# Shifted slices for the previous block's keys, and DMA copies for its values, in a fused attention and MLP kernel

## The chip, the cores and the metric

The kernel runs on one core of a Trainium2 chip. The metric is device time in microseconds (us) of one execution. A ratio is from the fast runs of both kernels in the same rounds, so it is not quite the ratio of the medians quoted beside it. Brackets hold a 95% interval. Where a ratio is turned into us, it is multiplied by 217.

The engines are called PE (matmuls), DVE (VectorE), ACT (ScalarE), POOL (GpSimd) and SP (SyncE, which here only issues DMAs). A profile is one execution, with its own span; its times differ a little from the medians.

## The reference

The kernel computes windowed attention with global keys, and a two-layer MLP over its result.

```python
# q, k, v: (4, 8, 768, 64); 8 global keys; a window of 96 keys
rel = pos[:, None] - pos[None, :]
is_global = pos[None, :] < n_global
is_local = (rel >= 0) & (rel < n_local)
dist = where(is_global & ~is_local, n_local, abs(rel))
scores = q @ k.T / sqrt(64) - slopes * dist        # -1e9 outside global and local
a = softmax(scores)
x = (a @ v)                                        # -> (3072, 512)
h = x @ w_in                                       # (512, 2048)
g = s * relu(h) ** 2 + b
out = g @ w_out                                    # (2048, 512), f32
```

## The kernel before

The work is cut into 12 granules of 256 tokens, three for each batch element (granules 0, 1, 2 are batch element 0; granules 0, 3, 6 and 9 are first in theirs). A granule is two blocks of 128 queries. A block needs its own 128 keys, and the keys of the block in front of it. The 8 global keys are put into that second set, in place of 8 keys that no query of the block can reach. So for each granule that is not the first of its batch element, DVE builds two patched copies: `koff` (keys, transposed) and `voff` (values, with a column of ones).

```python
def make_koff(j, blocks=range(GB), ...):
    ...
    copy(ko[:, i0:i0+n, hs, :], t[:, 0, r0+i0:r0+i0+n, hs, :])
    nc.vector.tensor_copy(ko[:, i0:i0+n, hs, 0:NG],
        t[:, 0, 0, hs, 0:NG].unsqueeze(1).to_broadcast((P, n, nh, NG)))

def make_voff(j, blocks=range(GB), ...):
    ...
    copy(vo[:, i0:i0+n, :, :], vn[:, r0+i0:r0+i0+n, :, :])        # L349
    for i in blocks:
        nc.vector.tensor_copy(vo[0:NG, i, :, :], vn[0:NG, 0, :, :])  # L353
```

The keys and queries of granules 4 and later are transposed by DMAs on SP's queue, four a granule. Everything is put in order by hand. This is the part around granules 4 and 5, which the argument is about; `p1` and `p2` are the two MLP layers, `scores(s)` are score matmuls, and `stage_A(u)` are value matmuls of one pair of heads (granule 4 has u = 16 to 19).

```python
# ... granule 2 and granule 3
qk_by_dma(4); load_scalars()
# ...
stage_A(11)
# ...
qk_by_dma(5)          # four transposes on SP's queue, each after its load
r0, q0 = p1_mm(2, 5)
r0()
stage_A(14)
stage_A(15, ps_h)
q0()
make_koff(4)
# ...
run(scores(8))        # granule 4's first scores
make_voff(4)
p2_mm(2, 0, 0, FC // 2)
# ...
step(8, ...)          # holds stage_A(16), the first reader of granule 4's voff
```

The softmax here doesn't subtract the row's maximum and nothing guards it: scores larger than these inputs give would overflow.

## Time and profile before

The kernel takes 216.85 us (median; 216.78 to 217.0).

| | before |
|---|---|
| span of the profiled run | 215.4 us |
| PE busy | 209.8 us (97%) |
| DVE busy | 140.5 us (65%) |
| time PE waited for anything | 2.1 us, 1.9 of it before 5.1 us |
| DVE work that the change takes out | 14.6 us |

First, the page of the kernel before: its span, the busy us of each engine, and three rows of digits. Each digit is a fortieth of the span, in tenths; PEclk is the clock granted to PE, and DMA the busy share of the 16 DMA engines.

```profile
span 215.4 us, 4939 instructions
...
PE 209.8 (97%) x2013; PEld 143.8 (67%) x2013; DVE 140.5 (65%) x344; ACT 113.6 (53%) x175; POOL 67.0 (31%) x89
...
PE   6999999999999999999999999999999999999993
...
PEclk9999999999999999999999999999999999999999
DMA  5999999999999997999999949952310310311102
```

PE is busy from end to end, and the DMA engines are full for the first half.

The waits of PE (the instruction that waited and what released it, us in total, times, longest) say the same. This is all that the view lists:

```profile
PE ps_w L155 <- DVE idle L145: 1.2, 1, 1.2
PE ps_t L269 <- DVE nat L233: 0.7, 1, 0.7
PE ps_av L446 <- DVE xn L420: 0.2, 1, 0.2
```

The DVE work that the change removes, from the groups of instructions (line, operation, operands, shapes and count; then busy us and the mean ns of one; then the idle time before):

```profile
L353 DVE COPY voff<-vb 8x528 bf16<-8x528 bf16 x16 | 4.8, 330 | 0.3
L349 DVE COPY voff<-vb 128x1056 bf16<-128x1056 bf16 (+1 forms) x9 | 4.2, 464 | 0.0
L330 DVE COPY koff<-qk 128x1024 bf16<-128x1024 bf16 (+1 forms) x9 | 3.5, 390 | 0.0
...
L333 DVE COPY koff<-qk 128x64 bf16<-128x64 bf16 (+1 forms) x9 | 2.1, 234 | 0.3
```

The place where granule 4's values are first read, in the chain that ended last (start, us, what). PE goes from one piece to the next with no gap:

```profile
64.97 1.83 PE ps L611 x8
66.80 0.24 PE ps_av L446 x8
67.05 1.76 PE ps L566 x16
```

And two stretches as sums (the busy us and instructions of each engine, the mean granted clock, the DMA share, which is not used here, and GB/s):

```profile
68.70:74.70 6.00, 5.96 (x56) 3.65 (x56) 4.57 (x12) 3.62 (x5) 1.21 (x2) 1.00 2.05 158
74.70:81.50 6.80, 6.80 (x75) 4.94 (x74) 4.18 (x10) 4.17 (x6) 0.00 (x0) 1.00 1.69 177
```

### The profile page before, as it was taken

What the parts mean: (1) busy time and instruction counts of PE and PEld (TensorE: products, weight loads), DVE (VectorE), ACT (ScalarE), POOL (GpSimd) and SP (SyncE); (2) the same over time, 40 slices, a digit from 0 to 9 for tenths busy, and PEclk for the clock granted to TensorE, in tenths of its full rate; (3) what the DMA queues carried; (4) which work ended last, traced back from release to release, by engine and by line L of the source; (5) the groups of instructions that cost most, each with busy time, mean ns of one, the idle gap of its engine ahead of it and who ended that gap; (6) DMA issues with size and microseconds to landing.
All of it is one profiled execution on the core that took longest, in us unless ns stands there. A gap on an engine that the chain in (4) does not pass through costs nothing.

```text
span 215.4 us, 4939 instructions
## 1 busy us (share of the span) xinstructions
PE 209.8 (97%) x2013; PEld 143.8 (67%) x2013; DVE 140.5 (65%) x344; ACT 113.6 (53%) x175; POOL 67.0 (31%) x89
## 2 busy tenths in 40 slices
PE   6999999999999999999999999999999999999993
PEld 2578885557866575776676676676676676665852
DVE  3497579995989668985675675666676663432421
ACT  4675668585975564554644643544644642240610
POOL 8873335897646104506318045000000000000000
PEclk9999999999999999999999999999999999999999
DMA  5999999999999997999999949952310310311102
GB/s 166 197 177 206 207 206 173 152 152 127 117 150 138 157 183 110 156 255 171 208 133 171 171 79 159 132 102 72 97 50 5 97 52 24 73 52 49 49 3 97
DMA packets 107079, 27.33 MB, mean 127 GB/s; under 512 B 97712, under 2 KB 104112, under 8 KB 107056
## 3 DMA queue, kind: packets, MB, share of 16 engines
q0 software_dynamic: 72864, 12.85, 82.2%
q1 hardware_dynamic: 33136, 13.64, 34.5%
q10 hardware_dynamic: 1056, 0.52, 0.9%
q8 instruction: 16, 0.26, 0.5%
q14 instruction: 7, 0.06, 0.1%
HBM read 27.26 MB, written 6.29 MB: 156 GB/s over the span
## 4 chain that ended last, share of the span: by engine, by line
PE 91%; DVE 5%; DMA 2%; issue 0%
PE ps L566 38%; PE ps L611 35%; PE ps_s L395 5%; PE ps_av L446 5%; DMA first<-in_k_dram 2%; PE ps_2c L668 2%; DVE pt L411 1%; PE ps_t L269 1%; PE ps_s L372 1%; PE ps_w L155 1%; PE ps_s L468 1%; PE ps_x L542 1%; PE ps_t L301 1%; DVE o_early L644 1%; DVE wsum L589 1%; DVE xn L420 1%
## 5 line engine op out<-in xcount | busy, mean ns | idle before, releaser
L576 ACT ACTIVATE gT<-ps 128x512 bf16<-128x512 f32 x96 | 57.0, 598 | 76.4 <-PE ps L566 76.4
L566 PE MATMUL ps<-xT,w_in_bf 128*128 128x256 bf16 x768 | 90.2, 273 | 0.0
L611 PE MATMUL ps<-w_out_bf,gT 128*128 128x512 bf16 x368 | 83.9, 380 | 0.0
L566 PEld LDWEIGHTS <-w_in_bf 128*128 128x128 bf16 x768 | 72.7, 98 | 8.9
L611 PEld LDWEIGHTS <-gT 128*128 128x128 bf16 x368 | 34.4, 98 | 39.2
L579 DVE TENSOR_TENSOR gT<-gT 128x512 bf16<-128x512 bf16 x96 | 40.4, 424 | 24.2 <-ACT gT L576 22.2
L404 ACT ACTIVATE pt<-ps_s 128x1024 bf16<-128x1024 f32 (+1 forms) x44 | 39.2, 948 | 6.4 <-PE ps_s L395 6.4
L411 DVE TENSOR_TENSOR pt<-pt,tmpl 128x1024 bf16<-128x1024 bf16 (+1 forms) x40 | 25.6, 650 | 9.3 <-ACT pt L404 8.6
L104 POOL DMA_DIRECT2D nat<-in_k_dram x22 | 19.7, 895 | 8.1 <-DMA w_in_bf<-in_moe_w_in_dram 3.0
L104 POOL DMA_DIRECT2D nat<-in_q_dram x22 | 19.6, 891 | 8.3 <-DMA w_out_bf<-in_moe_w_out_dram 3.4
L105 POOL DMA_DIRECT2D vb<-in_v_dram x22 | 19.8, 900 | 5.7 <-DMA w_out_bf<-in_moe_w_out_dram 2.1
L420 DVE TENSOR_TENSOR xn<-ps_av,rc 128x256 bf16<-128x256 f32 x48 | 20.4, 425 | 1.7
L622 DVE SCALAR_TENSOR_TENSOR o_sb<-ps,s_bc,bvec 128x512 f32<-128x512 f32 x19 | 14.1, 744 | 9.9 <-PE ps L611 9.9
L446 PEld LDWEIGHTS <-pt 128*128 128x128 bf16 x320 | 14.6, 97 | 5.9 <-DVE xn L420 0.8
L419 DVE RECIPROCAL rc<-ps_av 128x4 f32<-128x4 f32 x48 | 8.5, 178 | 14.8 <-PE ps_av L446 13.5
L446 PE MATMUL ps_av<-vb,pt 128*128 128x65 bf16 x208 | 15.4, 193 | 0.4 <-DVE xn L420 0.2
L110 POOL COPY gate<-xT 1x1 bf16<-1x1 bf16 x6 | 1.2, 202 | 40.6 <-DMA xT<-xn 37.9
L446 PE MATMUL ps_av<-voff,pt 128*128 128x65 bf16 x112 | 10.5, 193 | 0.0
L395 PE MATMUL ps_s<-qk 64*128 64x128 bf16 x208 | 10.0, 224 | 0.0
L589 DVE TENSOR_TENSOR wsum<-wsum,w_out_bf 128x512 f32<-128x512 f32 x14 | 9.6, 686 | 0.2
L395 PEld LDWEIGHTS <-qk 64*128 64x128 bf16 x208 | 6.2, 96 | 5.3 <-issue 3.2
L155 PE MATMUL ps_w<-idle 128*128 128x256 bf16 (+1 forms) x19 | 5.2, 434 | 1.2 <-DVE idle L145 1.2
(77 smaller groups left out, 107.6 us busy)
## 6 DMA issues: line engine op xcount, KB each, us to landing
out_dram<-o_sb SPq DMA_DIRECT2D x19, 256.0 KB, 3.5
nat<-in_k_dram POOLq DMA_DIRECT2D x22, 128.0 KB, 7.5
nat<-in_q_dram POOLq DMA_DIRECT2D x22, 128.0 KB, 7.4
vb<-in_v_dram POOLq DMA_DIRECT2D x22, 128.0 KB, 7.5
w_in_bf<-in_moe_w_in_dram POOLq DMA_DIRECT2D x4, 512.0 KB, 11.6
w_out_bf<-in_moe_w_out_dram POOLq DMA_DIRECT2D x4, 512.0 KB, 17.9
out_dram<-o_early SPq DMA_DIRECT2D x4, 256.0 KB, 6.6
first<-in_q_dram ACTq DMA_DIRECT2D x2, 256.0 KB, 4.9
```

The costliest lines, as they stand in the source:

```text
L104: nc.gpsimd.dma_start(t[:, n, i, :, :], rows_of(srcs[n], b, sb))
L105: nc.gpsimd.dma_start(vbuf[b % 2][:, sb, :, 0:D], rows_of(v, b, sb))
L395: nc.tensor.matmul(ps[:, hi, oc * P : (oc + 1) * P], lhsT=kt[rows], rhs=qt[rows], start=not bias, stop=not bias or part * GB + n == len(pl ...
L404: nc.scalar.activation(pt[:, :, 0:ncol], ps[:, :, 0:ncol], ACT.Exp, scale=QSCALE)
L411: nc.vector.tensor_tensor(pv, pv, m.rearrange("p h a c -> p h (a c)"), ALU.mult)
L420: nc.vector.tensor_tensor(dst, av[:, :, :, 0:D], rc[:].to_broadcast((P, 2, 2, D)), ALU.mult)
L446: nc.tensor.matmul(av[:, i, hi, 0 : D + 1], lhsT=pt[:, hi, c * P : (c + 1) * P], rhs=vv, start=(n == 0), stop=(n == len(terms) - 1),)
L566: nc.tensor.matmul(ps[:, i, :], lhsT=w_in_bf[:, kc, fc * P : (fc + 1) * P], rhs=xT[j][:, kc, :], start=(kc == 0), stop=(kc == KC - 1),)
L576: nc.scalar.activation(gs, ps[:], ACT.Relu)
L579: nc.vector.tensor_tensor(gs, gs, gs, ALU.mult)
L611: nc.tensor.matmul(po[:], lhsT=gT[j][:, fc, tb * P : (tb + 1) * P], rhs=w_out_bf[:, fc, :], start=(fc == 0), stop=(fc == FC - 1),)
L622: nc.vector.scalar_tensor_tensor(out=o_sb[:], in0=po_cur.pop((j, tb))[:], scalar=s_bc[:], in1=bvec[:], op0=ALU.mult, op1=ALU.add,)
```

## The change

The intent is to take the patched copies off DVE. For the keys, the 8 global keys are written once behind each 128-key block, in a strip of columns, so the previous block with its patch is simply the slice that starts 8 columns later. Small DVE copies (`attach`) fill the strips. The values have their keys on the partitions, where no such slice is possible; their copies stay, shifted by 8 rows, but two SP DMAs do them: one of 120 rows, one of the 8 global rows. The bias template gains a block for the shifted order.

```diff
-            qk[b] = qkp.tile([P, 2, NB, HP, P], BF16, name="qk", tag="qk")
+            qk[b] = (
+                qkp.tile([P, NB, HP, P + (NG + 15) // 16 * 16], BF16, name="kx", tag="kx"),
+                qkp.tile([P, NB, HP, P], BF16, name="qx", tag="qx"),
+            )
+    def k_off(b, r, hp):
+        return qk[b][0][:, r, hp, NG : P + NG]
+    def attach(b, lo, hi):
+        kx = qk[b][0]
+        nc.vector.tensor_copy(kx[:, lo:hi, :, P : P + NG],
+            kx[:, 0, :, 0:NG].unsqueeze(1).to_broadcast((P, hi - lo, HP, NG)))
+    def load_voff(j, blocks=range(GB)):
+        ...
+        nc.sync.dma_start(vo[0 : P - NG, i0 : i0 + n], vn[NG:P, r0 + i0 : r0 + i0 + n])
+        nc.sync.dma_start(
+            vo[P - NG : P, i0 : i0 + n], vn[0:NG, 0].unsqueeze(1).to_broadcast((NG, n, H, VW)))
-    def make_koff(...)      # and make_voff: removed, with their calls
 ... (template, order of blocks in the score plan, names: cut)
     cast_v(1, cp)
+    load_voff(1, [0])
     open_scores((2, 3))
+    load_voff(1, [1])
 ...
-    make_koff(2)
-    make_voff(2)
+    attach(0, 3, NB)
+    load_voff(2)
 ...
     stage_A(14)             # qk_by_dma(5) stands in front of this
+    load_voff(4)
     stage_A(15, ps_h)
     q0()
-    make_koff(4)
+    attach(1, 1, NB)
 ...
     run(scores(8))
-    make_voff(4)
 ... in step(), for granules 5 and later:
+        if not last and QK_PE < j + 1 < NJ:
+            load_voff(j + 1)
```

More of the change, by code (lines that the diff above doesn't have):

```diff
@@ L191 @@
     )
+    base_bf = const.tile([P, 4, P], BF16, name="base_bf")
     ident_bf = const.tile([P, P], BF16, name="ident_bf")
@@ L195 @@
     load_granule(1)
+    nc.gpsimd.affine_select(
+        out=base_bf[:, 3, :],
+        in_=rel[:, P - NG : 2 * P - NG],
+        pattern=[[0, P]],
+        compare_op=ALU.is_ge,
+        fill=-float(NL),
+        base=P - NG - 1,
+        channel_multiplier=-1,
+    )
     for i in range(4):
@@ L201 @@
     load_granule(3)
-    base_bf = const.tile([P, 3, P], BF16, name="base_bf")
-    nc.vector.tensor_copy(base_bf[:, 0, :], rel[:, 0:P])
-    nc.vector.tensor_copy(base_bf[:, 1:3, :], rel[:].rearrange("p (a c) -> p a c", a=2))
-    nc.vector.tensor_scalar_max(base_bf[0:NG, 0, :], base_bf[0:NG, 0, :], -float(NL))
-    nc.vector.memset(base_bf[0:NG, 2, :], -float(NL))
+    nc.vector.tensor_copy(base_bf[:, 0, :], rel[:, P : 2 * P])
+    nc.vector.tensor_copy(base_bf[:, 1, :], rel[:, 0:P])
+    nc.vector.tensor_copy(base_bf[:, 2, :], rel[:, 0:P])
+    nc.vector.memset(base_bf[0:NG, 0, :], -float(NL))
+    nc.vector.tensor_scalar_max(base_bf[0:NG, 1, :], base_bf[0:NG, 1, :], -float(NL))
     slopes = [float(2.0 ** (-8.0 * (h + 1) / H)) for h in range(H)]
@@ L219 @@
     diagonal(range(0, 4))
-    tmpl = const.tile([P, H, 5, P], BF16, name="tmpl")
+    tmpl = const.tile([P, H, 6, P], BF16, name="tmpl")
     def template(hs):
         for h in hs:
-            nc.scalar.activation(tmpl[:, h, 0:3, :], base_bf[:, 0:3, :], ACT.Exp, scale=slopes[h])
+            nc.scalar.activation(tmpl[:, h, 0:4, :], base_bf[:], ACT.Exp, scale=slopes[h])
     def template_rest(hs):
-        nc.vector.tensor_copy(tmpl[:, hs, 3, :], tmpl[:, hs, 2, :])
-        nc.scalar.copy(tmpl[:, hs, 4, :], tmpl[:, hs, 1, :])
+        nc.vector.tensor_copy(tmpl[:, hs, 4, :], tmpl[:, hs, 3, :])
+        nc.scalar.copy(tmpl[:, hs, 5, :], tmpl[:, hs, 2, :])
     def cast_first(h2, n, copy):
@@ L243 @@
     qk = {}
-    koff = {}
-    voff = {}
+    vb_off = [const.tile([P, GB, H, VW], BF16, name=f"vo{i}", tag=f"vo{i}") for i in range(2)]
     xn = {}
@@ L253, in unit, with qk_of, voff_of @@
         return j, hp, b, g
-    def qk_tile(b):
+    def qk_of(b, n):
         if b not in qk:
-            qk[b] = qkp.tile([P, 2, NB, HP, P], BF16, name="qk", tag="qk")
-        return qk[b]
+            qk[b] = (
+                qkp.tile([P, NB, HP, P + (NG + 15) // 16 * 16], BF16, name="kx", tag="kx"),
+                qkp.tile([P, NB, HP, P], BF16, name="qx", tag="qx"),
+            )
+        return qk[b][n][:, :, :, 0:P]
+    def k_off(b, r, hp):
+        return qk[b][0][:, r, hp, NG : P + NG]
+    def attach(b, lo, hi):
+        kx = qk[b][0]
+        nc.vector.tensor_copy(
+            kx[:, lo:hi, :, P : P + NG],
+            kx[:, 0, :, 0:NG].unsqueeze(1).to_broadcast((P, hi - lo, HP, NG)),
+        )
+    def voff_of(j):
+        return vb_off[j % 2]
+    def load_voff(j, blocks=range(GB)):
+        b, g = divmod(j, NGR)
+        if g == 0:
+            return
+        r0 = g * GB - 1
+        vn = vbuf[b % 2]
+        i0, n = blocks[0], len(blocks)
+        vo = voff_of(j)
+        nc.sync.dma_start(vo[0 : P - NG, i0 : i0 + n], vn[NG:P, r0 + i0 : r0 + i0 + n])
+        nc.sync.dma_start(
+            vo[P - NG : P, i0 : i0 + n], vn[0:NG, 0].unsqueeze(1).to_broadcast((NG, n, H, VW))
+        )
     def qk_by_pe(j, h2s=range(HP // 2), evac=(nc.vector.tensor_copy, nc.vector.tensor_copy)):
         b, g = divmod(j, NGR)
-        t = qk_tile(b)
         for h2 in h2s:
@@ L273, in qk_by_pe @@
                         )
-                dst = t[:, n, g * GB : (g + 1) * GB, 2 * h2 : 2 * h2 + 2, :]
+                dst = qk_of(b, n)[:, g * GB : (g + 1) * GB, 2 * h2 : 2 * h2 + 2, :]
                 if j == 0:
@@ L285, in qk_block @@
         b, g = divmod(j, NGR)
-        t = qk_tile(b)
         for n in range(2):
@@ L292, in qk_block @@
                 )
-            evac[n](t[:, n, g * GB + i, :, :], ps[:])
+            evac[n](qk_of(b, n)[:, g * GB + i], ps[:])
     def qk_wide(j, n, evac):
         b, g = divmod(j, NGR)
-        t = qk_tile(b)
         ps = ps_h.tile([P, GB, HP, P], BF16, name="ps_t", tag="psh")
@@ L303, in qk_wide @@
                 )
-        evac(t[:, n, g * GB : (g + 1) * GB, :, :], ps[:])
+        evac(qk_of(b, n)[:, g * GB : (g + 1) * GB], ps[:])
     def qk_by_dma(j):
         b, g = divmod(j, NGR)
-        t = qk_tile(b)
         for i in range(GB):
@@ L311, in qk_by_dma @@
                 nc.sync.dma_start_transpose(
-                    t[:, n, g * GB + i, :, :],
+                    qk_of(b, n)[:, g * GB + i],
                     nat[j][:, n, i, :, :].rearrange("p h d -> p (h d)"),
                 )
-    def make_koff(j, blocks=range(GB), h2=None, copy=nc.vector.tensor_copy, splice=True):
-        b, g = divmod(j, NGR)
-        if g == 0:
-            return
-        r0 = g * GB - 1
-        t = qk_tile(b)
-        if j not in koff:
-            koff[j] = work.tile([P, GB, HP, P], BF16, name="koff", tag="koff", bufs=2)
-        ko = koff[j]
-        hs = slice(0, HP) if h2 is None else slice(2 * h2, 2 * h2 + 2)
-        nh = HP if h2 is None else 2
-        i0, n = blocks[0], len(blocks)
-        if copy:
-            copy(ko[:, i0 : i0 + n, hs, :], t[:, 0, r0 + i0 : r0 + i0 + n, hs, :])
-        if not splice:
-            return
-        nc.vector.tensor_copy(
-            ko[:, i0 : i0 + n, hs, 0:NG],
-            t[:, 0, 0, hs, 0:NG].unsqueeze(1).to_broadcast((P, n, nh, NG)),
-        )
-    def make_voff(j, blocks=range(GB), copy=nc.vector.tensor_copy, splice=True):
-        b, g = divmod(j, NGR)
-        if g == 0:
-            return
-        r0 = g * GB - 1
-        vn = vbuf[b % 2]
-        if j not in voff:
-            voff[j] = work.tile([P, GB, H, VW], BF16, name="voff", tag="voff", bufs=2)
-        vo = voff[j]
-        i0, n = blocks[0], len(blocks)
-        if copy:
-            copy(vo[:, i0 : i0 + n, :, :], vn[:, r0 + i0 : r0 + i0 + n, :, :])
-        if not splice:
-            return
-        for i in blocks:
-            nc.vector.tensor_copy(vo[0:NG, i, :, :], vn[0:NG, 0, :, :])
     def stage_S(u):
         j, hp, b, g = unit(u)
-        t = qk_tile(b)
+        kv, qv = qk_of(b, 0), qk_of(b, 1)
         first = g == 0
@@ L367, in stage_S @@
         assert not bias or first
-        c0 = 0 if first else 1
+        c0 = 0 if first else 2
         def add_bias():
@@ L378, in add_bias @@
                 )
-        plan = [(i, t[:, 0, r0 + i, hp, :], t[:, 1, r0 + i, hp, :]) for i in range(GB)]
+        plan = [(i, kv[:, r0 + i, hp, :], qv[:, r0 + i, hp, :]) for i in range(GB)]
         if first:
-            plan.append((2, t[:, 0, 0, hp, :], t[:, 1, 1, hp, :]))
+            plan = [(1,) + plan[0][1:], (2,) + plan[1][1:], (0, kv[:, 0, hp, :], qv[:, 1, hp, :])]
         else:
@@ L386, in stage_S @@
                 (3,) + plan[1][1:],
-                (1, koff[j][:, 0, hp, :], t[:, 1, r0, hp, :]),
-                (2, koff[j][:, 1, hp, :], t[:, 1, r0 + 1, hp, :]),
+                (1, k_off(b, r0 - 1, hp), qv[:, r0, hp, :]),
+                (2, k_off(b, r0, hp), qv[:, r0 + 1, hp, :]),
             ]
@@ L435, in stage_A @@
             xn[j] = xpool.tile([P, GB, DM], BF16, name="xn", tag="xn")
-        dcol, ocol = ((0, 1), (None, 2)) if first else ((0, 3), (1, 2))
+        dcol, ocol = ((1, 2), (None, 0)) if first else ((0, 3), (1, 2))
         for i in range(GB):
@@ L441, in stage_A @@
                 if not first:
-                    terms.append((ocol[i], voff[j][:, i, h, 0 : D + 1]))
+                    terms.append((ocol[i], voff_of(j)[:, i, h, 0 : D + 1]))
                 elif i == 1:
-                    terms.append((2, vn[:, 0, h, 0 : D + 1]))
+                    terms.append((ocol[i], vn[:, 0, h, 0 : D + 1]))
                 for n, (c, vv) in enumerate(terms):
@@ L460, in block_S @@
         b, g = divmod(j, NGR)
-        t = qk_tile(b)
+        kv, qv = qk_of(b, 0), qk_of(b, 1)
         sb = g * GB + i
@@ L470, in block_S @@
                     lhsT=diag[:, 4 * pr + 2 * n + hi, :],
-                    rhs=base_bf[:, 1:3, :],
+                    rhs=base_bf[:, 2:4, :],
                     start=(n == 0),
@@ L478, in scores @@
                 hp = 2 * pr + n
-                for o, kt in enumerate((t[:, 0, sb, hp, :], koff[j][:, i, hp, :])):
+                for o, kt in enumerate((kv[:, sb, hp, :], k_off(b, sb - 1, hp))):
                     for hi in range(2):
@@ L485, in scores @@
                             lhsT=kt[rows],
-                            rhs=t[rows, 1, sb, hp, :],
+                            rhs=qv[rows, sb, hp, :],
                             start=False,
@@ L506, in block_A @@
                     h = 4 * pr + 2 * n + hi
-                    for o, vv in enumerate((vbuf[b % 2][:, g * GB + i, h], voff[j][:, i, h])):
+                    for o, vv in enumerate((vbuf[b % 2][:, g * GB + i, h], voff_of(j)[:, i, h])):
                         c = 2 * n + o
@@ L719, in step @@
             qk_by_dma(j + 2)
+        if not last and QK_PE < j + 1 < NJ:
+            load_voff(j + 1)
         run(scores(s + 1))
-        if not last and j not in voff:
-            make_voff(j)
         run(c0)
@@ L725, in step @@
         flush()
-        if not last and QK_PE <= j + 1 < NJ:
-            make_koff(j + 1)
+        if not last and j % NGR == 0:
+            attach(j // NGR, 1, NB)
         run(c1)
@@ L767 @@
     cast_v(0, cp)
-    make_koff(1, [0])
+    attach(0, 1, 3)
     cast_v(1, cp)
+    load_voff(1, [0])
     open_scores((2, 3))
+    load_voff(1, [1])
     qk_block(1, 0, (cp, cp))
@@ L780 @@
     x_by_pe(0, (cp, cp))
-    make_koff(1, [1])
     qk_block(1, 1, both)
@@ L786 @@
     s1()
-    make_voff(1, [0])
-    make_voff(1, [1])
     block_A(1, 0)
@@ L840 @@
     run(s5)
+    load_voff(3)
     qk_by_dma(4)
```

## The prediction

> **What bounds the kernel now.** TensorE. The page has PE busy for 209.8 of 215.4 us; the chain that ended last is 91% PE, and the waits list only 2.1 us of idle time before PE, 1.9 of it before 5.1 us. 16 matmuls of 512 columns take 3.45 to 3.56 us, 16 of 256 take 1.75, back to back from about 20 us to the end. DVE is 65% busy; its 5% of the chain lies under a PE that still works (7.43 of 7.50 us busy from 40.5 to 48 us). One mid-kernel wait of PE on DVE shows, 0.25 us at 88.2 us.
>
> **What goes.** On DVE (groups by form): key copies 3.5 us, key splices 2.1, value copies 4.2, value splices 4.8: 14.6 us. In their place come six copies of 64 to 160 elements per partition, an estimated 1.6 us (64 elements now take 0.18). DVE should fall from 140.5 to about 127.5 us. ACT pays an estimated 0.9 us for four template blocks instead of three. PE's matmuls keep number, shape and order. So almost all of the saving is off the critical path: I give it 0.3 us.
>
> **What comes.** Value shifts become pairs of SP-queue DMAs, 270 KB per granule. An unloaded 256 KB store lands in 2.0 us, but the engines are 90% busy until about 125 us, and a transpose that lands in 2.4 us unloaded takes 7 to 9.5 between 47 and 72 us.
>
> 1. Granule 1 (issued about 11.3 us, needed at 16.95): should just land.
> 2. Traffic. A 2 KB packet took 86 to 95 ns, so a shift costs all 16 engines an estimated 0.8 us and delays queued loads by that. The last block of granule 2's q landed at 40.47 us and is used at 40.8. Estimate: 0.5 us of PE wait.
> 3. Granule 4, the main loss. Its DMA stands on the SP queue behind granule 5's four transposes; the last is issued at 61.38 us, when its load lands, and lands at 69.26. A transfer issued behind four transposes landed 0.8 us after the last of them (62.23 after 61.38; 79.52 after 78.77). The Trainium skill ("DMA: Bandwidth & Descriptors", Queues, rings and completion order) says each engine consumes a ring in order, which fits. So the values land at about 70.2 us, with delayed loads nearer 71.5. PE wants them at 66.80. PE waits 4 us or more, and, saturated afterwards, never recovers.
>
> A wait this long may also slow the clock: the skill ("TensorE: Matmul & The Clock Gate", part 1) gives half rate after an idle window of about 3.4 us. The trace shows half-rate matmuls only in its first 10 us. I add 0.8 us for the chance.
>
> Granules 5, 7 and later have an estimated 1.5 us or more in hand.
>
> **Predicted time.** 216.85 - 0.3 + 4.6 (total delay of PE up to granule 4) + 0.8 = 221.9 us, 8 in 10 between 217.6 and 224.5. Chances: faster by over 2%: 0.03; within 2%: 0.41; slower by over 2%: 0.56.
>
> **What would show it.** DVE near 127 us; PE's waits naming the value-shift DMA, 3 to 5 us, just before granule 4's first value matmul (near 67 us); the rest of the schedule shifted by that much. If right about the clock, 512-column matmuls of 0.43 us just after.
>
> **What would make it wrong.** If the shift overtakes the transposes or these land sooner, the wait shrinks to 0 to 2 us and the time stays within 1%. A late shift in granules 1, 2 or 7 would add. A faster kernel needs PE waits that the profile doesn't show.

## The result

The changed kernel takes 227.48 us (226.64 to 228.4) against 216.85; the ratio is 1.0485 [1.0454, 1.0516]. It is slower by about 10.5 us, which is outside the predicted range. It passes the comparison with the reference. (That comparison does not test the shifted order: it also passes two kernels below that are wrong.)

The page of the kernel after, the same lines as above:

```profile
span 225.3 us, 4923 instructions
...
PE 210.4 (93%) x2013; PEld 144.2 (64%) x2013; DVE 129.8 (58%) x307; ACT 114.4 (51%) x175; POOL 67.0 (30%) x90
...
PE   6797999999982799999999999999999999999994
...
PEclk9999999999999599999999999999999999999999
DMA  6999999999999991699999998955241220311102
```

PE has the same 2013 matmuls and the same busy time within 0.6 us, but there is a hole in slices 12 to 14, where the digits 8, 2, 7 stand in place of nines, and the clock's digit is 5 in slice 14. The 7 in slice 4 is a smaller one, near 18 us. DVE fell by 10.7 us. The longest waits of PE now name the value copies:

```profile
PE ps_av L444 <- DMA vo<-vb: 5.8, 1, 5.8
PE ps_av L507 <- DMA vo<-vb: 1.6, 1, 1.6
PE ps_w L155 <- DVE idle L145: 1.2, 1, 1.2
PE ps_s L393 <- DMA qx<-nat: 0.8, 1, 0.8
...
```

L507 reads granule 1's values and L444 those of the later granules (the wait of 5.8 us is granule 4's); L393 are granule 4's scores, which read query transposes done by DMA. The chain that ended last shows how the long one comes about:

```profile
51.74 11.55 DMA nat<-in_q_dram
...
63.31 1.24 SPq L349
...
64.64 0.90 SPq L297
...
65.59 9.05 DMA vo<-vb
...
74.69 0.57 PE ps_av L444 x7
75.26 3.41 PE ps L564 x16
```

Read it from the top. A load of granule 5's queries lands at 63.29 us. Only then can SP issue granule 5's fourth transpose (L349), and only behind that the two copies of granule 4's values (L297 and L298, at 64.64 and 65.59). The second lands at 74.64, 9.05 us after its issue, and PE starts at 74.69. (A landing is the last of the semaphore increments that the trace records for a DMA.) The 16 matmuls after it take 3.41 us where they took 1.76. The stretches show the same hole and the slow clock behind it, a mean of 0.81 and then 0.67:

```profile
68.70:74.70 6.00, 0.25 (x3) 0.02 (x2) 0.74 (x2) 0.24 (x1) 2.63 (x3) 0.81 1.70 169
74.70:81.50 6.80, 6.80 (x64) 5.29 (x65) 3.06 (x8) 2.28 (x4) 0.00 (x0) 0.67 1.99 153
```

Both kernels have the same matmuls in the same order, so the delay of each can be read: its start after, less its start before.

| where | start before, us | start after, us | delay, us | added here |
|---|---|---|---|---|
| granule 1, first shifted value | 16.99 | 18.12 | 1.13 | 1.13 |
| granule 4, scores after the query transposes | 61.60 | 63.69 | 2.09 | 0.96 |
| granule 4, first shifted value | 66.67 | 74.69 | 8.02 | 5.93 |
| a first-layer matmul, the clock just full again | 69.19 | 79.11 | 9.92 | 1.90 |
| last matmul | 211.85 | 221.78 | 9.93 | 0.01 |

After 79 us nothing is added and nothing given back. (In the opening this profile of the changed kernel ran up to 1.8 us ahead and still had 0.5 in hand at 11 to 16 us, because its clock came up sooner: 384-column matmuls start 0.16 us apart from 5.8 us on, while those of the kernel before are 0.32 apart at 6 to 7 us and 0.16 only from about 10. The first experiment below tells whether that belongs to the change.)

So the theory is that DVE's saving buys nothing, and that the whole loss is value copies that land late: mostly granule 4's, then the slow clock which its wait brings, and about 2 us from the copies in the first 65 us. The rivals are the key layout, a cost of the copies wherever they stand, and a slow clock that only looks like a cost.

### The profile page after: what moved, and what is told of

It is laid out like the page before. It is cut to its first block, busy times and chain, and to the rows that moved or that the text cites. A ratio compares the mean times of both kernels' runs of the same rounds, so it can differ in the third digit from the quotient of the medians.

```text
span 225.3 us, 4923 instructions
## 1 busy us (share of the span) xinstructions
PE 210.4 (93%) x2013; PEld 144.2 (64%) x2013; DVE 129.8 (58%) x307; ACT 114.4 (51%) x175; POOL 67.0 (30%) x90
## 4 chain that ended last, share of the span: by engine, by line
PE 77%; DMA 16%; POOL 2%; DVE 2%; SPq 1%; issue 0%; POOLq 0%
PE ps L564 34%; PE ps L609 32%; DMA vo<-vb 8%; DMA nat<-in_q_dram 5%; PE ps_av L444 4%; PE ps_s L393 4%; DMA nat<-in_k_dram 3%; PE ps_2c L666 2%; POOL nat L104 1%; DVE o_early L642 1%; DVE xn L418 1%; SPq L349 1%; PE ps_av L507 0%; DVE pt L409 0%; SPq L297 0%
## 5 line engine op out<-in xcount | busy, mean ns | idle before, releaser
L564 PE MATMUL ps<-xT,w_in_bf 128*128 128x256 bf16 x768 | 92.0, 276 | 0.0
L564 PEld LDWEIGHTS <-w_in_bf 128*128 128x128 bf16 x768 | 73.8, 99 | 9.5
L444 PEld LDWEIGHTS <-pt 128*128 128x128 bf16 x320 | 14.9, 99 | 11.7 <-DMA vo<-vb 6.1
L444 PE MATMUL ps_av<-vo,pt 128*128 128x65 bf16 x112 | 10.7, 197 | 5.8 <-DMA vo<-vb 5.8
L444 PE MATMUL ps_av<-vb,pt 128*128 128x65 bf16 x208 | 15.8, 195 | 0.2 <-DVE xn L418 0.2
L393 PE MATMUL ps_s<-qx,kx 64*128 64x128 bf16 x320 | 13.0, 217 | 1.0 <-DMA qx<-nat 0.8
L393 PEld LDWEIGHTS <-kx 64*128 64x128 bf16 x320 | 9.2, 94 | 6.1 <-issue 5.1
```

Source lines behind the costliest of these rows:

```text
L393: nc.tensor.matmul(ps[:, hi, oc * P : (oc + 1) * P], lhsT=kt[rows], rhs=qt[rows], start=not bias, stop=not bias or part * GB + n == len(pl ...
L444: nc.tensor.matmul(av[:, i, hi, 0 : D + 1], lhsT=pt[:, hi, c * P : (c + 1) * P], rhs=vv, start=(n == 0), stop=(n == len(terms) - 1),)
L564: nc.tensor.matmul(ps[:, i, :], lhsT=w_in_bf[:, kc, fc * P : (fc + 1) * P], rhs=xT[j][:, kc, :], start=(kc == 0), stop=(kc == KC - 1),)
```

## The experiments

Twelve kernels were run, each against the kernel before in the same rounds. Two of them, `keys_only` and `copies_unread`, compute something wrong. Their times count, their results do not.

### Each half alone

`keys_only` is the changed kernel with the values copied by DVE again, at the old places. The copies are not shifted, so the value rows do not match the key order (wrong).

```diff
-    load_voff(4)
...
     run(scores(8))
+    make_voff(4)          # and so for the other granules: DVE, as before
```

> Key half alone: shifted-slice keys and the new template layout stay, the value copies are made by VectorE as before (they are not shifted, so the result is wrong on purpose). Theory (late value DMAs make the loss, the key layout costs nothing): about 216.3 us, 0.6 below before, since the opening reaches the first value matmul of granule 1 at 16.4 us in place of 17.0 once the key copies are gone. Rival (the padded key layout, the strided evacuations or the longer template cost time): 218 us or more.

Measured: 217.00 us against 217.02; ratio 0.9992 [0.9975, 1.0008]. The key half costs nothing and gains nothing (the 0.6 us that I expected did not come), and the lead of the opening is gone: in this profile the clock came up at 10.4 us (by the clock records of the trace file), so the lead was the phase of the clock in one profile. DVE's busy time in it is 136.7 us, down from 140.5, and PE takes no notice.

`values_only` is the kernel before with the values copied by SP DMAs where the change has them. The rows stay in the old order, so the result is right.

```diff
+        nc.sync.dma_start(vo[NG:P, i0 : i0 + n], vn[NG:P, r0 + i0 : r0 + i0 + n])
+        nc.sync.dma_start(vo[0:NG, i0 : i0 + n], vn[0:NG, 0].unsqueeze(1).to_broadcast(...))
...
     stage_A(14)
+    load_voff(4)
...
-    make_voff(4)
```

> Value half alone: the kernel before with its value copies made by the same SP-queue DMAs at the same places (unshifted, so the result is right). Theory: about 227 us (226 to 228.5), the same wait of 5 to 6 us before granule 4's first value matmul and slow 256-column matmuls after it. Rival (the keys are the loss): within 1 us of 216.85.

Measured: 226.92 us; ratio 1.0445 [1.0413, 1.0476]. Its waits:

```profile
PE ps_av L444 <- DMA vo<-vb: 6.1, 2, 5.6
...
PE ps_av L507 <- DMA vo<-vb: 1.5, 1, 1.5
```

The value half is the loss; the two intervals overlap with that of the whole change. The shift itself (8 rows) has no part in it that these runs resolve.

### The copies without the waits for them

`copies_unread` issues all copies of the change, but the value matmuls read the unpatched values (wrong). Only the copies' traffic and their issue on SP are left.

```diff
-                    terms.append((ocol[i], voff_of(j)[:, i, h, 0 : D + 1]))
+                    terms.append((ocol[i], vn[:, g * GB + i - 1, h, 0 : D + 1]))
```

> The changed kernel with all its value DMAs issued, but the value matmuls read the unshifted V in their place (wrong result on purpose). It keeps the traffic and the queue time and takes away the wait for the landing. Theory: 216.3 plus about 0.8 us for loads that the traffic delays, about 217.1 us. Rival (the copies' traffic itself slows loads, stores and transposes by as much as the loss): 222 us or more.

Measured: 218.42 us; ratio 1.0061 [1.0036, 1.0086], that is 1.3 us, above my 217.1 and well below the rival's 222. So some 9 us of the 10.5 are waits for the copies and what follows from them. The rest is the traffic: in this run PE waited on other transfers, which the profile before has no wait for.

```profile
PE ps L564 <- DMA xT<-xn: 1.1, 2, 1.0
PE ps L609 <- DMA w_out_bf<-in_moe_w_out_dram: 0.4, 1, 0.4
```

### Granule 4's copy: where it is issued

`shift4_earlier` moves one call, ahead of granule 5's four transposes.

```diff
     stage_A(11)
+    load_voff(4)
 ...
     stage_A(14)
-    load_voff(4)
```

> The changed kernel with one line moved: granule 4's value shift is issued after the value matmuls of unit 11, so that on the SP queue it stands before granule 5's four transposes instead of behind them. Theory: it is issued near 58 us instead of 64.6, lands near 66, and both the 5.8 us wait and the slow clock behind it go: about 219 us (218 to 220), 2 us over before. Rival (any transfer at that time is late because the DMA engines are full): a wait of 3 us or more stays, 223 us or more.

Measured: 220.83 us; ratio 1.0171 [1.0149, 1.0194]. It gives back 3.1% (1.0485 less 1.0171), or 6.8 us, so this one place is two thirds of the loss. The copies are issued 6.1 us earlier, the clock stays at 1.0 throughout the profiled run (the slowest of the four, 221.31 us, had a mean of 0.992), and no wait for granule 4's values is left:

```profile
58.51 0.91 SPq L297 DMA_DIRECT2D vo<-vb  x1
59.46 0.80 SPq L298 DMA_DIRECT2D vo<-vb  x1
```

They landed at 66.67 and 68.19, 8.2 and 8.7 us after issue, although none of granule 5's transposes stood in front of them; behind those the same two took 9.3 and 9.1 us. Standing behind the transposes made the copies late mostly because they were *issued* late, not because they took longer. But this does not compare a copy behind transposes with a copy behind none: here granule 4's four stood in front, the last of them issued at 54.03 and landed at 63.83.

The trace file also holds every DMA packet with its queue, time and size, which no view prints one by one. In the changed kernel, granule 4's 120 rows (packets of 2112 bytes) begin to move at 71.04 us, 6.4 us after their issue; the 256-byte packets of the transposes issued before them end at 71.30. Granule 2's 120 rows, issued at 38.98 with nothing else in flight on SP's queue, begin 4.0 us after their issue and land after 7.3 us, while GpSimd's loads fill the engines. And in the next run below those loads pause: none of their packets runs from 74.0 to 77.5 us, and granule 5's copy, issued at 74.76 on SP's queue behind transposes still in flight, lands after 3.65 us. So most of the flight goes with GpSimd's loads, and the place behind the transposes adds about 2.4 us before the rows move (an estimate: 6.4 less 4.0). This is read from the packets; no run was made to test it.

The time is just above the stated range, so somewhat more stays than I thought. What PE waits for now:

```profile
PE ps_s L393 <- DMA qx<-nat: 1.7, 2, 0.9
PE ps_av L507 <- DMA vo<-vb: 1.4, 1, 1.4
```

`shift4_act_queue` was to tell order on SP's queue from full DMA engines: granule 4's copies at the same place in the program, from ACT's queue.

```diff
-        nc.sync.dma_start(vo[0 : P - NG, ...], ...)      # likewise the second copy
+        eng.dma_start(vo[0 : P - NG, ...], ...)          # eng = nc.scalar for granule 4
```

> The changed kernel, with granule 4's value shift issued at the same place in the program but from ScalarE's DMA queue. It does not stand behind the transposes in program order or in their ring, but goes out into equally full engines, near 61.5 us. Theory (its place on the SP queue is the main cause): landing near 69, a wait of at most 1.5 us, no slow clock, 219 to 221 us. Rival (full engines alone): landing after 72, 224 us or more.

Measured: 231.05 us; ratio 1.0656 [1.0634, 1.0679]. A miss, and it does not answer its question. ACT did not issue the copy until 70.39 us and stood idle for it, so ACT's own work, and then PE, waited (ACT's timeline, then the longest of PE's waits):

```profile
70.39 1.47 ACTq L297 DMA_DIRECT2D vo<-vb  x1
71.97 0.79 ACTq L298 DMA_DIRECT2D vo<-vb  x1
72.81 1.09 ACT L574 ACTIVATE gT<-ps 128x512 bf16<-128x512 f32 x2 [11.87 <-DMA nat<-in_k_dram]
...
PE ps_x L540 <- ACT gT L574: 10.8, 1, 10.8
```

The profile infers a load as the releaser. The semaphore that this copy used had last been used by granule 5's third transpose, issued at 61.26 and landed at 70.29, which is 0.10 us before the copy's issue; so I take it that the issue waited for that transpose to land. That is read from the times and was not tested. Once issued, the copies landed in 5.5 and 4.6 us, in the stretch in which GpSimd's loads pause. What part of the 9 us behind the transposes is order on SP's queue is therefore not told by this run; the 2.4 us above are the best estimate.

### The slow clock: cost or symptom

`fill_the_wait` is the changed kernel, with 50 idle matmuls of 256 columns in the place where PE waits for granule 4's values.

```diff
-    step(8, [lambda: rest(2, 0)], p1[3][0:2], p1[3][2:4])
+    step(8, [lambda: rest(2, 0), lambda: warm(50)], p1[3][0:2], p1[3][2:4])
```

> The changed kernel with 50 idle matmuls of 256 columns (about 5.4 us of PE work) put just before granule 4's first value matmul, inside the 5.8 us wait. The data lands when it did. Theory (the idle PE drops to half clock, which costs about 2 us after the wait): the clock stays up, the 16 matmuls of 256 columns after the wait take 1.75 us instead of 3.41, and the time falls by 1.5 to 2 us to about 225.6. Rival (what follows the wait is slow for another reason): 227.5 or more.

Measured: 225.24 us; ratio 1.0381 [1.0362, 1.0401], so *adding* 5.6 us of useless matmuls made the kernel 2.3 us faster (1.0485 less 1.0381, times 217). In its timeline the 16 matmuls after the wait are at full speed again (the timeline's 1.91 us includes the end of the last; the same entry of the changed kernel is 3.60):

```profile
69.17 5.62 PE L155 MATMUL ps_w<-idle 128*128 128x256 bf16 x50
...
74.87 1.91 PE L564 MATMUL ps<-xT,w_in_bf 128*128 128x256 bf16 x16
```

The slow clock is a cost of its own, and the idle PE its cause.

### What stays with granule 4's copy early

`shifts_earlier` adds to `shift4_earlier` what could help granule 1: the second block of V is loaded and cast first, its 120-row copy is issued at once, and the two 8-row copies are merged.

```diff
-    for i in range(GB):
+    for i in (1, 0):                 # order of the first V loads
...
+    load_voff(1, [0], glob=False)
     attach(0, 1, 3)
+    cast_v(0, cp)
+    load_voff(1, local=False)
```

> The kernel with granule 4's shift moved, and granule 1's shift made earlier too: V block 1 is loaded and cast before block 0, its shifted copy is issued at once (near 8.5 us in place of 10.1), and the two small copies of global rows become one. Theory (each late shift costs its own wait): granule 1's wait of 1.4 us falls under 0.5, the late q transposes of granule 4 (1.7 us in two waits) stay: 1 to 1.5 us under the kernel with only granule 4 moved, 219.3 to 219.8. Rival (the early copies only push loads back by as much): no gain, 220.8.

Measured (five rounds): 219.99 us; ratio 1.0141 [1.0128, 1.0155]. This is a miss: about 0.7 us below `shift4_earlier`, with intervals that overlap, and granule 1's wait was still 1.4 us in its profile. But there the copy was issued at 11.24 us and not near 8.5 (it landed at 18.90), so this profile does not try what an early issue does. Its clock came up at 10.6 us, and the copy follows the opening: with the old opening it was issued at 11.2 to 11.7 us in three profiles whose clock came up at 9 to 10 us, and at 10.1 to 10.4 in four where it came up at 4 to 5.

`shifts_earlier_v_last` adds that from granule 4 on, keys and queries are loaded before values, so that the transposes get their data sooner. `before_v_last` is the control: the kernel before with that order.

```diff
+            if j < 4:
                 nc.gpsimd.dma_start(vbuf[b % 2][:, sb, :, 0:D], rows_of(v, b, sb))
+        for i in range(GB if j >= 4 else 0):      # the V loads, after all of K and Q
+            sb = g * GB + i
+            nc.gpsimd.dma_start(vbuf[b % 2][:, sb, :, 0:D], rows_of(v, b, sb))
```

> As the last one, and from granule 4 on each granule's four loads of k and q are issued before its two of v. Theory (granule 4's transposes are late because the copies' traffic delays its loads): the wait of PE on q transposes falls from 1.7 us to under 0.5, the time to 217.3 to 218.5, near before but not under it, since VectorE's relief was never on the critical path. Rival (another cause of the late transposes): the wait stays and the time is within 0.5 us of the last one.

> Control: the kernel before with the same load order and nothing else. It shows no wait of PE on transposes, so theory expects 217.0, within 0.3 us of before. If it is faster by more, part of what the reordered version gains has nothing to do with the change.

Measured (five rounds): 219.97 us, 1.0138 [1.0124, 1.0152], and the control 216.99 us, 0.9998 [0.9985, 1.0012]. The first is a miss: the order of loads gave nothing in time. In its profile, whose clock came up at 4.8 us, granule 1's copy was issued at 9.38 and landed at 16.01, before PE wanted it at 16.55, and that wait is gone; but the waits only moved to other transfers, a weight load among them:

```profile
PE ps_s L399 <- DMA qx<-nat: 1.1, 2, 0.8
PE ps L570 <- DMA w_in_bf<-in_moe_w_in_dram: 0.9, 1, 0.9
```

Three more kernels split what stays. All three are the kernel before with unshifted value copies, DVE for some granules and SP DMAs for the others, so their results are right.

```diff
 # dma_1_2_only:        load_voff for granules 1 and 2, make_voff (DVE) for the others
 # dma_4_early_only:    load_voff for granule 4, after stage_A(11); make_voff for the others
 # dma_from_granule_5:  make_voff for granules 1, 2 and 4; load_voff for the others
```

> Edit: the kernel before, with its key copies and unshifted values; only granules 1 and 2 have their values copied by SyncE DMAs, issued where the change issues them; all the others by VectorE at the old places. Result stays right. Theory (the 3 us that stay when granule 4's wait is removed come from the copies of the opening: granule 1's wait, and loads and transposes that land late behind the copies' 1 MB): 219.3 (218.6 to 220.0), with a PE wait on granule 1's values of 1 to 2 us and one on granule 4's query transposes of 0.4 us or more. Rival (the residual comes from the copies of granule 4 and later): 217.5 or less.

> Edit: the kernel before, with its key copies and unshifted values; only granule 4's values are copied by SyncE DMAs, issued early, between stages 11 and granule 2's finish, ahead of granule 5's four transposes; all other granules by VectorE at the old places. Result stays right. The pieces found so far: 1.7 us for granules 1 and 2 alone, 0.4 for granule 5 and later alone, 3.1 to 3.9 for all copies with granule 4's moved early. Theory (granule 4's copy still costs when it is early, because granule 5's transposes land behind it and PE waits for them with granule 5's scores, as it did 0.9 us in the version with the early issue): 218.0 (217.6 to 218.5), with a PE wait on granule 5's transposes of 0.4 us or more. Rival (early, it costs nothing by itself, and the rest of the 3.1 us comes of the copies adding up in the same engines): 217.3 or less.

> Edit: the kernel before, with its key copies and unshifted values; granules 1, 2 and 4 have their values copied by VectorE at the old places, granules 5, 7, 8, 10 and 11 by two SyncE DMAs each. Result stays right. Theory (copies cost only in the first 75 us, where the DMA engines are full and PE depends on what lands; later they land in about 3 us, long before they are wanted): 217.0 (216.7 to 217.4), no PE wait on a value copy. Rival (each DMA copy takes something from PE wherever it stands, so the residual of about 3 us is spread over all seven): 218.5 or more.

| kernel | median, us | ratio | in us |
|---|---|---|---|
| `dma_1_2_only` | 218.72 | 1.0090 [1.0072, 1.0107] | 2.0 |
| `dma_4_early_only` | 217.96 | 1.0050 [1.0009, 1.0090] | 1.1 |
| `dma_from_granule_5` | 217.43 | 1.0023 [1.0003, 1.0042] | 0.5 |
| their sum | | 1.0163 | 3.5 |
| `shift4_earlier` (all, one early) | 220.83 | 1.0171 [1.0149, 1.0194] | 3.7 |

The three parts add up to the whole within their intervals, so no interaction between them is needed. One run carries much of the second: of the six of `dma_4_early_only` five took 217.18 to 218.27 us, and one 220.43 with a mean clock of 0.992; without it 0.6 us would be left of the 1.1. All three rivals fall. The third came out just above the expected range: the copies of granule 5 and later cost 0.5 us and gain nothing. Granule 5's pair still stands in a full stretch (issued at 72.13 and 73.17 in the kept trace) and took 8.4 and 7.6 us to land; the one at 145 us took 3.2 and 2.5. Of `dma_1_2_only` and `dma_from_granule_5` I read one profile, of spans 216.5 and 216.2 us, and the kept trace is of another, of 218.1 and 215.3. The waits that bear on the copies and that the kernel before has not, from the profiles that I read, `dma_1_2_only` first, then `dma_4_early_only`, then `dma_from_granule_5`:

```profile
PE ps_av L524 <- DMA vo<-vb: 1.6, 1, 1.6
...
PE ps_av L461 <- DMA vo<-vb: 0.3, 1, 0.3
```

```profile
PE ps_s L410 <- DMA qk<-nat: 1.0, 1, 1.0
```

```profile
PE ps L581 <- DMA xT<-xn: 0.7, 1, 0.7
```

The kept traces, again `dma_1_2_only` (a wait, then part of the chain) and `dma_from_granule_5`:

```profile
PE ps_av L524 <- DMA vo<-vb: 1.7, 1, 1.7
...
18.59 0.61 PE ps_av L524 x15
19.20 1.67 PE ps_w L155 x8
20.87 1.71 PE ps L581 x8
```

```profile
PE ps L581 <- DMA xT<-xn: 0.2, 1, 0.2
```

Granules 1 and 2 cost by their own landings (in the kept trace granule 1's two 120-row copies were issued at 11.26 and 13.18 and landed at 18.55 and 19.67), and in some executions by the clock as well: after the wait of 1.7 us the granted clock was 0.50 from 19.1 to 22.5 us, and each group of 8 matmuls in it took 1.7 us, against 0.87 in the kernel before. That execution is 1.6 us longer than the other. The wait for granule 4's query transposes that I expected there is in neither profile. Granule 4's copy, even early, costs through something else: granule 5's transposes land later, and PE waits 1.0 us for them, the qk wait of the second fence. With granule 5's copies it is another transpose, that of the attention's result (xT), for which PE waits 0.7 us in one profile and 0.2 in the other.

No version tried beats the kernel before. The one that keeps a part of the change for nothing is the key layout of `keys_only`, which is no faster; it would also need the value copies in the shifted order to be right, which was not tried without DMAs.

## Why the prediction was wrong

The direction, the mechanism and the place were right. The size was not: I had 5.1 us (221.9 less 216.85) and the loss is 10.5, with the upper end of the range at 224.5. The step that failed is the time from issue to landing that I gave to a value copy in items 1 and 3 (granule 4's pair landed at 74.64 us, not at 70.2 to 71.5; granule 1's took 7.95 us and did not just land), and with it the 0.8 us for the clock. Term by term, against the delays of the profile:

| term of the sum | predicted, us | measured, us |
|---|---|---|
| DVE's saving on the critical path | -0.3 | 0 (`keys_only` 0.9992) |
| granule 1's copy | 0 ("should just land") | 1.1 (wait of 1.6; delay 1.13) |
| traffic of the copies, up to granule 4's scores | 0.5 | 1.0 (0.96) |
| granule 4's copy | 4.1 | 5.9 (5.93) |
| slow clock after it | 0.8 | 1.9 (2.3 by `fill_the_wait`) |
| sum | 5.1 | 9.9 of span |

**DVE.** "So almost all of the saving is off the critical path" was right; it was all of it. The 14.6 us of removed groups were read correctly, and the groups' sum fell by 13.2 (150.0 to 136.8), but DVE's busy time fell only by 10.7, to 129.8 and not to 127.5: the durations of neighbouring DVE instructions overlap, so a sum of groups is more than busy time (150.0 against 140.5 before). It mattered nothing here.

**Granule 1** was the plainest failure. "Issued about 11.3 us, needed at 16.95: should just land" left 5.6 us. The issue was even earlier, at 10.13, and the copies still landed at 18.08 and 18.82, because they took 7.95 and 6.8 us. I had costed a copy by an unloaded store (2.0 us) in a stretch whose DMA digit is 9, while quoting in the same sentence that a transpose takes 7 to 9.5 us under such a load (between 47 and 72 us). That was the number to use. An earlier issue can mend this wait (9.38 us in the profile of `shifts_earlier_v_last`), but other waits took its place there.

**Traffic.** The 0.5 us were right in kind and named the wrong place. There was no wait at 40.8 us: PE already came 1.1 us late and the load was there. The delay appeared at 63.69 instead, where granule 4's last query transpose landed at 63.65 and not at 61.38. `copies_unread` puts the traffic alone at 1.3 us.

**Granule 4.** "Its DMA stands on the SP queue behind granule 5's four transposes" is what the chain shows, and `shift4_earlier` confirms it by giving back 6.8 us. The landing was mis-sized: "about 70.2 us, with delayed loads nearer 71.5", measured 74.64. Of the 4.4 us, 1.9 came of the load that held the fourth transpose (landed at 63.29, not at 61.37), and 0.9 of that transpose's own longer flight (8.73 us, not 7.88). The other 1.7 is the step from its landing to the copy's: I took 0.8 to 0.9 us from transfers that follow four transposes, and it was 2.6 (72.04 to 74.64). I left out two things: that SP is held for each issue (about 1.2 us or more for a transpose, as the trace before shows; 0.90 and 1.52 for these two), and that the time from issue to landing is 7 to 9.5 us for whatever is issued there, which the trace before shows too. From the corrected issue of the second copy, 65.59, a landing between 72.6 and 75.1 would have followed. PE itself was 2.1 us late by then, which hid a part of it: the wait is 5.8 and not 7.9.

On the Trainium skill's "DMA: Bandwidth & Descriptors" (Queues, rings and completion order), which I cited for order on a ring: the packets agree, since granule 4's rows begin to move at 71.04 us, as those of the transposes issued before them end (71.30). But order is the smaller part, for a copy with nothing in front of it on SP's queue took 7.3 us. The same section says that each DMA engine takes turns between the queues it has work for. That would fit copies which are slow because another queue is full, as would the 3.65 us where GpSimd's loads paused, but no run here isolates it.

**The clock.** "I add 0.8 us for the chance" weighted a cost that then came in full. The skill ("TensorE: Matmul & The Clock Gate", Part 1) says half rate after an idle window of about 3.4 us, with windows that run freely. The changed kernel's trace agrees: the granted clock fell 3.5 us into the wait of 5.8, the 16 matmuls after it took 3.41 us against 1.76, a factor of 1.94, and full rate was back some 4.5 us after PE resumed. The cost is half of the time at half rate, here half of 4.5 us. The kept trace of `dma_1_2_only` differs from the page: there a wait of 1.7 us was enough, while waits of 1.4 to 1.6 us at the same place, in six other profiles, brought no slow clock. The measurement decides: a wait shorter than the window can bring the half rate, and how short is safe these runs do not show.

**The range.** All five terms erred in the same direction, and the landings of granules 1 and 4, with the clock that follows the second, rest on one number, the latency of a DMA in a full stretch. A range that treats them as independent is too narrow.

One thing stays open: how much of the copy's flight behind the transposes is order on SP's queue and how much full engines. `shift4_act_queue` did not answer it; the 2.4 us of order are an estimate from packets of two stretches, not a test.

## What to carry to other kernels

Work taken from an engine that was not the bottleneck was worth nothing here, and moving it onto DMA engines that were full cost whatever then waited for a landing; look at the DMA row of the page at the moment of the move, not at its mean. Cost a new transfer by the issue-to-landing time of transfers in the same stretch, and its issue by the last thing that holds the same issuing queue. A PE that waits can also pay for a slow clock afterwards (waits of 10.8 and 5.8 us brought it here, and in one execution a wait of 1.7 us; waits of 1.4 to 1.6 us did not), and once saturated it gave no delay back.

## What the Trainium skill lacked or had wrong

- "DMA: Bandwidth & Descriptors" (Anatomy of one DMA) puts the fixed cost of a DMA that GpSimd issues at about 2 us. For the SBUF-to-SBUF copies of 248 KB from SP's queue the runs show 3.2 to 3.4 us from issue to landing after 145 us, with the DMA engines mostly idle, but 7.3 to 9.3 us up to 80 us, with them full of GpSimd's loads (7.3 with nothing else on SP's queue). The time from issue to landing of such a copy beside a full queue is lacking.
- The same page (Why a DMA increments its semaphore by 16 and not by 1) was needed to read the landings, and agrees: the 120-row copies show 15 + 1 increments in the trace and the 8-row copies 8 + 1. Nothing to mend.
- "DMA: Bandwidth & Descriptors" has no issue time measured on this chip for such transfers (only cycle counts in a table that sets earlier chips against trn3). The runs show SP held for 0.65 to 1.0 us by most of these copies, 1.52 by one, and 1.2 to 1.4 by most transposes, in full and in empty stretches alike (0.76 and 0.88 at 155 us); later transfers of that queue were issued only after it.
- "TensorE: Matmul & The Clock Gate" (Part 1) agrees with the half rate after 5.8 us of idleness. Its idle window of about 3.4 us is not a safe limit, though: in one profile of `dma_1_2_only` the half rate followed a wait of 1.7 us. The price of one such event, 2.3 us by `fill_the_wait`, is a number worth adding there.
